# Forty zero products in TensorE's stream, an earlier memset, and a new written order, in an attention and feed-forward kernel

## The chip, the cores and the metric

The kernel runs on one core of one Trainium2 chip. The metric is the device time of one execution in microseconds, the median of several runs. The core has five engines, each with an instruction stream that it executes in order: TensorE (PE in the profile; its weight loads are shown apart as PEld), VectorE (DVE), ScalarE (ACT), GpSimd (POOL) and SyncE (SP). In this kernel POOL does little more than issue loads, SP issues transposes by DMA and stores.

## The reference: what is computed

Attention with a relative-position bias over 8 batches t, 8 heads, 576 positions and head size 64, and then a feed-forward layer over all 4608 positions:

```python
scores = scale * np.matmul(q, k.transpose(0, 1, 3, 2))   # (8, 8, 576, 576), head size 64
scores = scores + bias.transpose(2, 0, 1)[None, :, :, :] # by |distance| bucket and head
attn = softmax(scores)                                   # over the last axis
x = np.matmul(attn, v)  ->  (8 * 576, 512)               # heads side by side
h = x @ w_in                                             # (4608, 2048)
s = np.sin(alpha * h)
g = h + s * s / (alpha + 1e-09)
return g @ w_out                                         # (4608, 512), float32
```

The inputs are float32; the kernel works in float16 with float32 sums.

## The kernel before

**Tiles and stages.** Heads go in pairs p = 0..3, queries of a batch in two windows w of 256 and a rest of 64. The task names used below are those of the source; the digits are t, p, w, half, or block and slice.

- `n` (L581) loads a pair's k or q in natural order through POOL, casting it to float16; `t` (L703) turns it on TensorE, and `c` copies it to the tile kT or qT on DVE or ACT. The first pair comes in two halves by its own loads (`r`), casts (`f`, L653 on DVE or L651 on ACT), turns (`th`, L688) and copies (`ch`). From t = 3 on, k and q are staged in float16 in DRAM (`g`, L608, POOL) and turned by a DMA transpose on SP (`k`, L614). `v` (L587) and `y` (L593) load the values.
- `T` (L766) makes a group of four score products into two banks of PSUM; `X` (L720, L725, L749) and `S` do it for the rest of 64. `E` is the exp on ACT (L774), `B` the product with the bias band on DVE, `A` (L805, L810) and `L` (L821) the products with v, `N` the division (L842, L843). `Y` turns the result into the tile xT: for t = 0 on TensorE (`P`) with a copy, later by a DMA transpose on SP (L850, L861).
- The feed-forward layer goes in 9 blocks of 512 positions. `I` (L887) is one slice of 128 of the first product, four 128x512 products; `Z` (L893) the sine, `Q` the square, `G` (L905) the sum; `O` (L915) a piece of the second product, `W` the eviction and `D` the store. A block's `I` needs the `Y` of every batch that it covers.
- A bias table is made early: `bu`, `be`, `bs`, `bm`, `bc`, then `j` loads it as a band (tile toep, L662) on SP or POOL, and `m` makes masks from it.

**What sets the order.** One long string, ORDER, lists all tasks; `/` is followed by the engine, where it is not the first that the task allows (A is ACT, D is DVE, G is POOL), and the PSUM bank. `_planned` only checks it. Each engine's instructions come in exactly that order, and a task waits at its place for what it needs. The string begins:

```text
id/A r00 ms r10/A r01 n011 r11/A sub n020 cst tab al n021 n100 f00 n031 th00/7 f10/A ch00 n010 f01
th10/6 y00 th01/7 ch10 ch01/A T0000/0 v00 T0001/2 ET0000 n131 bu/7 ET0001 f11 t020/6 n030 be
```

Near the second batch's end it reads, around SP's transposes: `L2 ... Y23 ... YL2 ... Y20 ... k41 ... I2.0`.

**Cleared tiles.** Task `ms` (L569 to L578) writes constants on DVE: ones and zeros in the tiles of v and vt, and zeros in the two tiles kd. From t = 2 on, kd holds the last 64 columns of two heads' k as a block diagonal (`o`), so that one full product does for both heads.

Of the kernel before, what the change touches and what calls it, by code (L numbers as in the profile page):

```python
# [45 lines left out]
def _graph(K):  # L46
# [15 lines left out]
    ms = add("ms", "DVE", lambda e, b: K.memsets())  # L62
# [277 lines left out]
PE_X, KD = 1, 2  # L340
# [3 lines left out]
id/A r00 ms r10/A r01 n011 r11/A sub n020 cst tab al n021 n100 f00 n031 th00/7 f10/A ch00 n010 f01  # L344
th10/6 y00 th01/7 ch10 ch01/A T0000/0 v00 T0001/2 ET0000 n131 bu/7 ET0001 f11 t020/6 n030 be
th11/5 c020/A t021/4 bs n121 ch11 bm/7 c021/A n111 T0010/0 bc T0210/2 ET0010 j0 j2/G T0201/4
t011/7 ET0210 t010/6 j1/G c011 T0211/0 ET0201 T0200/2 j3 c010 at/7 n110 ET0200 av T0101/4 v03
t100/6 t031/7 ET0101 c100 t030/3 v01 t131/2 c031 ET0211 T0100/4 y01 c030 ET0100 v02 c131 T0300/0
X00r/6 ET0300 n101 BT0210 BT0200 T0110/2 t111/5 n231 BT0000 ET0110 T0011/0 n130 t121/4 BT0001 c111
ET0011 n200 X01r/2 BT0010 c121 m0 EX00r X00q/0 BT0201 BT0110 m1 BT0101 EX01r BT0100 X01q/4 wi1  # L350
T0311/6 BX00r EX01q BT0011 A000/3 n210 BT0300 A010/2 EX00q n220 N000 A001/5 m3 BT0211 ET0311
t110/4 N010 m2 t101/3 T0111/0 c110/A N001 T0301/6 n120 ET0111 BX01r T0310/4 c101 n230 A020/2
ET0301 BT0111 wi2 A021/3 N020 T1000/0 ET0310 wi0 S0/7 N021 t130/6 y11 t231/2 ET1000 BT0301 T1001/4
BX00q A011/3 BT0311 wi3 ES0 c231 c130/A X10r/0 y10 ET1001 A030/7 BT0310 N011 v12 P00/6 BS0 EX10r
P02/2 A031/3 N030 v11 BX01q T1011/4 Y02/A N031 t220/7 ET1011 n221 T1100/0 Y00 T1300/2 c220 P01/6
ET1100 P03/5 Y01 t120/4 BT1011 t210/7 ET1300 T1010/0 c120 L0/6 ET1010 Y03 wo0 t230/4 NL0 t200/5
T1311/2 c200 T1301/0 I0.8/6 ET1311 c230 ET1301 S1/5 c210 X11r/2 v10 I0.0/4 BT1000 EX11r BT1100 v13
I0.3/7 ES1 Z0.0 BS1 BT1010 I0.9/5 BT1300 PL0/3 I0.7/2 YL0 n211 Z0.9 Q0.0 I0.1/3 wo1 Z0.3 Q0.9 G0.0
Z0.7 I0.12/1 v21 Q0.3/A G0.9 I0.2/4 wo2 Z0.8 G0.3 Q0.7/A I0.5/5 n201 Q0.8 Z0.2 G0.7 I0.14/7 Z0.1
Q0.2 Q0.1/A G0.8 I0.10/2 Z0.12 wo3 G0.2 I0.13/6 Q0.12/A BX10r g31 G0.1 Z0.10 I0.4/4 BT1001 Z0.14  # L360
G0.12 A100/3 Q0.10/A Q0.14 I0.11/1 Z0.5 G0.10 g30 Z0.4 G0.14 I0.6/0 Q0.4/A BX11r Z0.11 N100
I0.15/7 G0.4 Q0.5/A y20 O0.0/3 Z0.6 G0.5 O1.0/2 g40 Q0.6/A O0.2 O0.4 Z0.15 G0.6 T1101/4 Z0.13 O1.2
Q0.11 ET1101 Q0.15 O0.6 G0.11 v22 A101/0 BT1301 O0.8 G0.15 A130/1 N101 O1.4 N130 Y10 O1.6 Q0.13
X11q/4 T1111/0 G0.13 t211/7 v20 ET1111 O1.8 c211 O0.10 y21 EX11q BT1111 T1200/0 O1.10 BT1311
ET1200 t201/7 t221/6 T1110/4 c221 T1201/0 ET1110 O1.12 BT1200 O1.14 ET1201 c201 O0.12 T1310/4 v23
W1 X10q/6 ET1310 T1210/0 BT1101 O0.14 BT1110 BX11q A110/2 BT1201 EX10q W0 A111/5 BT1310 D0 ET1210
N110 A120/4 N111 T1211/6 T2100/2 o2 T2110/0 ET1211 Y11 O3.0/5 BT1210 BX10q O3.2 ET2100 BT1211 O3.4
X20r/6 N120 ET2110 A131/3 S2/4 A121/2 EX20r N131 T2200/0 N121 O3.6 ES2 ET2200 BT2100 T2111/6 Y12
T2101/2 O2.0/4 ET2111 O3.8 X21r/0 ET2101 O3.10 Y13 O3.12 EX21r O3.14 T2000/2 k30 T2201/6 T2211/0
ET2000 O2.2 O2.4 ET2201 O2.6 O2.8 ET2211 BT2201 O2.10 BT2101 W3 T2001/2 T2210/6 T2010/0 BT2111  # L370
ET2001 D3 L1/5 BT2200 ET2010 I1.5/3 BX21r D1 v33 BX20r ET2210 T2310/0 v32 k31 I1.8/2 ET2310 y30
I1.1/7 Z1.5 g71 A210/6 I1.14/1 N210 Z1.8 NL1 I1.15/0 y31 Q1.8/A Q1.5 I1.0/6 G1.5 Z1.14 g50 Z1.1
I1.2/5 Q1.14 G1.8 Z1.0 I1.7/3 Q1.0/A BT2110 G1.14 v30 A220/2 G1.0 Z1.7 I1.13/1 g41 Q1.1/A N220
Z1.2 I1.6/6 G1.1 Q1.7/A Q1.2 I1.4/2 o3/A G1.7 Z1.6 I1.3/7 BT2000 Z1.4 G1.2 O2.12 Z1.15 O2.14 Q1.4
Q1.6/A I1.10/5 G1.4 g51 W2/A Q1.15 O5.0/3 Z1.3 G1.6 I1.12/4 Q1.3/A G1.15 Z1.13 I1.9/6 G1.3 Z1.10
O6.0/2 Q1.13 Z1.12 I1.11/7 G1.13 Z1.9 Q1.10 g60 X21q/0 Q1.9 Z1.11 O5.2 G1.10 EX21q O6.2 Q1.11 O5.4
BT2210 G1.9 A211/5 O5.6 G1.11 O6.4 BT2211 T2011/6 T2300/0 Q1.12 O6.6 ET2300 G1.12 O5.8 O6.8 N211
ET2011 O6.10 BT2010 Y21 BT2300 T2301/0 T2311/4 BT2011 T3110/6 O6.12 ET2311 BT2310 O5.10 BT2001
ET2301 O5.12 D2 O6.14 A200/5 ET3110 BT2301 O5.14 N200 W6/A T3300/0 YL1 T3011/6 W5 X20q/4 ET3300
A221/2 BS2 BT2311 O4.0/3 EX20q N221 O4.2 BT3300 T3301/0 ET3011 T3000/4 Y22 A201/2 BX21q ET3301  # L380
A230/7 N201 k40 A231/6 ET3000 N230 X30r/0 N231 O4.4 EX30r O4.6 BX20q T3001/4 L2/2 ET3001 Y23
T3101/0 NL2 v42 T3211/6 T3100/4 ET3101 O4.8 YL2 v41 O4.10 ET3100 O4.12 y41 O7.0/2 ET3211 BT3100
X31q/0 v31 T3111/4 O7.2 ET3111 Y20 g70 O7.4 O4.14 EX31q X30q/4 W4 T3201/6 O7.6 EX30q BT3011 k41
# [548 lines left out]
def kernel(  # L932
# [48 lines left out]
```

## Time and profile before

| | us |
|---|---|
| median of 3 runs | 381.02 |
| lowest and highest | 379.35, 384.81 |
| the profiled execution | 381.76 |
| its span, first to last instruction | 379.9 |
| PE, ACT, DVE, POOL busy in the span | 365.4, 310.5, 265.3, 86.0 |

The profile is one execution. A matmul's busy time is modelled from a pipeline, so a busy PE need not be at its peak. The slices are a fortieth of the span, 9.5 us, each; a digit is tenths of busy time, and for PEclk tenths of the full TensorE clock that was granted. In the list of waits a line gives who waited, what ended the wait, and us in total, times and longest. The chain follows the work that ended last back to the start; its rows give start, length and what was on it. In the timeline each row is a run of like instructions, with the idle time before it in brackets.

### The profile page before, as it was taken

The page shows a single profiled execution, that of the slowest core. Times are in us where ns is not written, and L with a number is a line of the kernel's source. Part 1 is how long each engine was busy: PE and PEld are TensorE (multiplying, and loading weights), DVE is VectorE, ACT ScalarE, POOL GpSimd, SP SyncE. Part 2 cuts the span into 40 slices and gives each one's busy share as a digit, 9 for nine tenths or more (in the row PEclk, how much of TensorE's full clock was granted, in tenths as well). Part 3 has the DMA queues.
Part 4 walks back from the last instruction along what each step waited for, and adds up shares of the span by engine and source line. Part 5 has one row for each costly group of instructions (what it writes and reads, how often), then busy time and mean ns, then how long its engine had stood idle before and what let it go on. Part 6 is the DMA issues. An engine that isn't in the chain of part 4 may idle for free.

```text
span 379.9 us, 9143 instructions
## 1 busy us (share of the span) xinstructions
PE 365.4 (96%) x3769; PEld 195.6 (51%) x3769; DVE 265.3 (70%) x613; ACT 310.5 (82%) x417; POOL 86.0 (23%) x104
## 2 busy tenths in 40 slices
PE   4879999999998899999999999999999999999996
PEld 3567445654464455544554555445654564444453
DVE  4789899639975496389754985596729866769412
ACT  5979998999899599899988989999899855686301
POOL 8894682048208000600000050500000000000000
PEclk9989999999999899999999999999999999999999
DMA  9999999999999992890254078980130032020005
GB/s 174 217 170 184 186 193 158 126 201 145 157 131 142 172 100 57 93 155 21 98 129 97 0 83 135 141 69 28 40 89 3 2 83 92 2 83 0 2 29 193
DMA packets 140889, 39.68 MB, mean 104 GB/s; under 512 B 126208, under 2 KB 136304, under 8 KB 140848
## 3 DMA queue, kind: packets, MB, share of 16 engines
q0 software_dynamic: 92864, 18.45, 60.0%
q1 hardware_dynamic: 46272, 18.61, 23.5%
q10 hardware_dynamic: 1712, 2.04, 1.6%
q8 instruction: 29, 0.48, 0.5%
q14 instruction: 12, 0.10, 0.1%
HBM read 36.89 MB, written 15.34 MB: 137 GB/s over the span
## 4 chain that ended last, share of the span: by engine, by line
PE 88%; DMA 6%; ACT 2%; POOL 1%; issue 1%; SPq 1%; DVE 1%; POOLq 0%
PE acc L915 33%; PE acc L887 31%; PE acc L810 8%; PE acc L766 8%; PE acc L805 2%; DMA xT<-xp 2%; DMA v<-in_v_dram 2%; PE acc L821 2%; DMA xT<-in_k_dram 2%; DMA toep<-e_sb 1%; ACT s L893 1%; PE acc L720 1%; PE acc L703 1%; POOL xT L581 1%; PE acc L749 1%
## 5 line engine op out<-in xcount | busy, mean ns | idle before, releaser
L915 PE MATMUL acc<-w_out,g 128*128 128x512 f16 (+1 forms) x592 | 144.3, 374 | 0.0
L887 PE MATMUL acc<-xT,w_in 128*128 128x512 f16 x576 | 135.8, 381 | 2.8 <-DMA xT<-xp 2.2
L774 ACT ACTIVATE u<-acc 128x1024 f16<-128x1024 f32 x128 | 123.7, 1034 | 12.2 <-PE acc L766 11.3
L893 ACT ACTIVATE s<-acc,alphaT 128x512 f16<-128x512 f32 x144 | 91.9, 682 | 23.6 <-PE acc L887 23.0
L905 DVE SCALAR_TENSOR_TENSOR g<-s,inv_a,acc 128x512 f16<-128x512 f16 x144 | 103.2, 742 | 7.3 <-ACT s L898 5.7
L887 PEld LDWEIGHTS <-w_in 128*128 128x128 f16 x576 | 55.3, 98 | 69.2 <-issue 6.5
L915 PEld LDWEIGHTS <-g 128*128 128x128 f16 x592 | 52.7, 98 | 59.0 <-issue 7.3
L797 DVE TENSOR_TENSOR u<-u,toep 128x256 f16<-128x256 f16 (+1 forms) x128 | 58.9, 489 | 19.8 <-ACT u L774 19.5
L587 POOL DMA_DIRECT2D v<-in_v_dram x32 | 30.9, 972 | 145.5 <-PE acc L821 79.0
L810 PE MATMUL acc<-v,u 128*128 128x65 f16 x1024 | 45.4, 196 | 0.5 <-DMA v<-in_v_dram 0.5
L900 DVE TENSOR_TENSOR s<-s 128x512 f16<-128x512 f16 x83 | 34.0, 419 | 17.0 <-ACT s L893 16.7
L810 PEld LDWEIGHTS <-u 128*128 128x128 f16 x1024 | 41.9, 99 | 4.9 <-issue 0.9
L766 PE MATMUL acc<-qT,kT 64*128 64x256 f16 x512 | 42.0, 278 | 1.5 <-DVE kT L653 1.0
L898 ACT ACTIVATE s<-s 128x512 f16<-128x512 f16 x61 | 37.9, 629 | 1.1
L653 DVE COPY outs<-acc 128x512 f32<-128x512 f32 (+1 forms) x24 | 16.2, 675 | 26.7 <-PE acc L915 25.4
L774 ACT ACTIVATE ux<-acc 128x1024 f16<-128x1024 f32 x32 | 32.4, 1035 | 1.8 <-PE acc L720 0.9
L766 PEld LDWEIGHTS <-kT 64*128 64x128 f16 x512 | 20.4, 96 | 22.8 <-issue 18.2
L842 DVE RECIPROCAL rden<-acc 128x4 f32<-128x4 f32 x72 | 12.7, 177 | 25.1 <-PE acc L810 18.7
L805 PE MATMUL acc<-vt,ux 128*128 128x130 f16 x128 | 28.8, 225 | 1.0 <-DMA vt<-in_v_dram 1.0
L843 DVE TENSOR_TENSOR xp<-acc,rden 128x256 f16<-128x256 f32 x64 | 27.2, 424 | 2.3
L651 ACT ACTIVATE outs<-acc 128x512 f32<-128x512 f32 (+1 forms) x13 | 7.6, 582 | 18.6 <-PE acc L915 18.5
L805 PEld LDWEIGHTS <-ux 128*128 128x128 f16 x128 | 12.7, 99 | 8.2 <-issue 2.8
(68 smaller groups left out, 199.2 us busy)
## 6 DMA issues: line engine op xcount, KB each, us to landing
out_dram<-outs SPq DMA_DIRECT2D x30, 256.0 KB, 2.3
v<-in_v_dram POOLq DMA_DIRECT2D x32, 128.0 KB, 6.8
staged_q<-in_q_dram POOLq DMA_DIRECT2D x5, 576.0 KB, 12.4
staged_k<-in_k_dram POOLq DMA_DIRECT2D x5, 576.0 KB, 14.9
w_in<-in_moe_w_in_dram POOLq DMA_DIRECT2D x4, 512.0 KB, 10.5
w_out<-in_moe_w_out_dram POOLq DMA_DIRECT2D x4, 512.0 KB, 10.6
xT<-in_q_dram POOLq DMA_DIRECT2D x11, 144.0 KB, 5.6
xT<-in_k_dram POOLq DMA_DIRECT2D x11, 144.0 KB, 5.9
```

What stands on the lines that cost most here:

```text
L587: self.nc.gpsimd.dma_start(out=self.vs[t % 2][:, c, :, 0:D], in_=src)
L766: self.nc.tensor.matmul(out=s[:, o:o + 256], lhsT=self.kT[t % 2][r, p, 128 * c:128 * c + 128], rhs=self.qT[t % 2][r, p, 256 * w:256 * w + ...
L774: self.nc.scalar.activation(out=c["u"], in_=c["s"], func=AF.Exp, scale=0.125)
L797: self.nc.vector.tensor_tensor(out=io, in0=io, in1=m, op=ALU.mult)
L805: nc.tensor.matmul(out=c["av"][:, 130 * j:130 * j + 130], lhsT=cx["u"][:, o:o + 128], rhs=vt[:, p, :], start=True, stop=True, skip_group_c ...
L810: nc.tensor.matmul(out=c["av"][:, 130 * j + 65 * a:130 * j + 65 * a + 65], lhsT=cells[ch // 2]["u"][:, o:o + 128], rhs=vv[:, ch, 2 * p + a ...
L887: self.nc.tensor.matmul(out=c["h"], lhsT=self.w_in[:, j, 128 * f:128 * f + 128], rhs=self.xT[:, j, 512 * b:512 * b + 512], start=(j == 0), ...
L893: self.nc.scalar.activation(out=c["s"], in_=c["h"], func=AF.Sin, scale=self.alphaT[:, f:f + 1])
L898: self.nc.scalar.activation(out=c["s"], in_=c["s"], func=AF.Square)
L900: self.nc.vector.tensor_tensor(out=c["s"], in0=c["s"], in1=c["s"], op=ALU.mult)
L905: self.nc.vector.scalar_tensor_tensor(out=self.g[b][:, f, :], in0=c["s"], scalar=self.inv_a[:, f:f + 1], in1=c["h"], op0=ALU.mult, op1=ALU ...
L915: self.nc.tensor.matmul(out=c["mo"], lhsT=self.g[b][:, f, 128 * (tau % 4):128 * (tau % 4) + 128], rhs=self.w_out[:, f, at], start=(f == 0) ...
```

## The change

Three things change. A new task `mz` clears the two kd tiles first, ahead of `ms`, which keeps the rest of the constants. Forty new tasks `F0` to `F39` on TensorE, which depend on `mz` alone, each multiply a cleared kd tile by itself into a free bank of PSUM, 512 columns wide; nothing reads the result. Depending on the task written before it on TensorE, a fill uses all of the array, one half of its rows, or half of its columns. And ORDER is written anew from its second word to its last: every engine's stream, the queues of SP and POOL and the banks follow another order, and some copies change between DVE and ACT (the first cast, f00, goes to ACT, the copy `bc` and the masks m0, m1, m3 to DVE).

```diff
-    ms = add("ms", "DVE", lambda e, b: K.memsets())
+    zero = add("mz", "DVE", lambda e, b: K.memset_kd())
+    ms = add("ms", "DVE", lambda e, b: K.memsets(), [zero])
+    for i in range(NFILL):
+        add(f"F{i}", "PE", lambda e, b: K.fill(b), [zero], bank=1)
...
-PE_X, KD = 1, 2
+PE_X, KD, NFILL = 1, 2, 40
...
+        self.form = "full"
...
+    def memset_kd(self):
+        for i in (1, 0):
+            self.nc.vector.memset(self.kd[i], 0.0)
...
-            self.nc.vector.memset(self.kd[i], 0.0)
+
+    def fill(self, bank):
+
+        z, o = self.kd[1], self.acc[:, bank, :]
+        if self.form == "rows":
+            z = z[64 * (bank % 2):64 * (bank % 2) + 64]
+        w = z[:, 0, 0:64] if self.form == "cols" else z[:, 0, :]
+        self.nc.tensor.matmul(out=o[0:64] if self.form == "cols" else o, lhsT=w,
+                              rhs=z[:, :, :].rearrange("p a n -> p (a n)"), start=True, stop=True)
...
+            if eng == "PE" and task.key[0] != "F":
+                k = task.key
+                rows = k[0] == "T" or k[0] == "X" and k[-1] == "q"
+                ops.form = "rows" if rows else "cols" if k[0] in "tL" else "full"
```

The new string begins as follows. It has six fills before the first turn, three more before the first score group T0000, 29 between that and the first A (A000), and two between A000 and the first product of the feed-forward layer, which is I0.2 in place of I0.8:

```text
id/A r00 mz r10/A r01 n021 ms F0/7 r11/A sub n011 F1/6 cst tab F2/7 al n020 F3/6 n010 F4/7 f00/A
F5/6 n031 th00/7 f10/A F6/6 n030 f01 th10/5 F7/6 n130 ch10 th01/4 ch00 F8/6 v01 ch01/A T0000/0
```

Around SP's transposes before block 2 it reads: `Y23 ... k40 ... Y22 ... k41 ... Y20 ... Y21 ... I2.10`, with v43, v40, g70 and g61 on POOL between Y20 and I2.10. Before block 7 it reads `Y73 ... I6.4 ... O22.14 ... L7 ... I7.3`.

More of the change, by code (lines that the diff above doesn't have):

```diff
@@ L349 @@
[L349 to L354, printed above, removed]
@@ L373 @@
[L373 to L378, printed above, removed]
@@ L379 @@
[L379 to L383, printed above, removed]
-S3/3 O7.8 g61 BT3000 ET3201 O7.10 BT3110 X31r/0 BX30r BX31q T3200/4 ES3 BT3001 EX31r T3010/6
@@ L460 @@
+O35.4a O35.8a D33 O32.14 O35.12a W32/A O35.4b W35a D32/A O35.8b D35a O35.12b W35b/A D35b/A
 """
```

216 lines of the change are left out of this document (117 added, 99 removed).

## The prediction

> **What bounds the kernel now.** I read the page first: the span and its 40 slices of 9.5 us each.
>
> ```profile
> span 379.9 us, 9143 instructions
> ...
> PE   4879999999998899999999999999999999999996
> ...
> PEclk9989999999999899999999999999999999999999
> ```
>
> TensorE is full but for two places: the first four slices, and a dip near slice 13. Both have a dip of the granted clock in or behind them. The list of PE's waits (us in total, times, longest) names them; its first row, 3.9 us, is the wait for the first load, shown below:
>
> ```profile
> PE acc L887 <- DMA xT<-xp: 2.2, 1, 2.2
> PE acc L805 <- DMA vt<-in_v_dram: 1.0, 1, 1.0
> ...
> PE acc L810 <- DMA v<-in_v_dram: 0.5, 1, 0.5
> ```
>
> The chain that ended last (start, length, what) says when PE becomes the bound:
>
> ```profile
> 1.29 3.26 POOL xT L581 x5
> ...
> 10.42 5.67 DMA toep<-e_sb
> ...
> 16.38 6.17 DMA v<-in_v_dram
> ...
> 22.59 0.45 PE acc L810 x6
> ...
> 25.34 0.44 PE acc L810 x8
> ...
> 28.22 0.24 PE acc L810 x8
> ...
> 29.33 0.63 PE acc L703 x24
> ...
> 36.22 0.74 PE acc L821 x34
> ...
> 118.21 6.32 DMA xT<-xp
> ...
> 165.34 11.22 PE acc L887 x52
> ```
>
> Up to 22.59 us the chain is POOL's loads: the last chunk of v for the first batch (t=0) holds the first A. After that it is nearly all TensorE. So the end moves by what changes before 22.59, by products added or taken behind it, and by the gap at 118 to 128. At full rate a 128x512 product is 11.22/52 = 0.216 us. The row at 25.34 shows A's products at 0.44 per eight, the row at 28.22 at 0.24: the stretch behind the v wait ran at half rate. The windows confirm it:
>
> ```profile
> 5.00:10.00 5.00, 4.57 (x62) 3.31 (x64) 1.63 (x5) 3.81 (x7) 4.28 (x7) 1.00 1.35 202
> 10.00:15.00 5.00, 4.64 (x99) 3.25 (x93) 3.03 (x7) 5.00 (x7) 4.42 (x7) 1.00 1.41 240
> 15.00:20.00 5.00, 3.58 (x64) 1.72 (x61) 4.89 (x11) 5.00 (x6) 4.35 (x8) 1.00 1.89 190
> 22.00:23.00 1.00, 0.46 (x10) 0.41 (x8) 1.00 (x3) 1.00 (x3) 1.00 (x3) 0.84 1.42 142
> 24.00:25.00 1.00, 1.00 (x21) 1.00 (x19) 1.00 (x3) 0.00 (x0) 0.92 (x3) 0.50 1.18 196
> 26.00:27.00 1.00, 1.00 (x32) 0.83 (x27) 0.96 (x4) 0.64 (x2) 1.00 (x2) 0.96 1.25 191
> 125.00:126.00 1.00, 1.00 (x5) 0.35 (x3) 0.00 (x0) 1.00 (x1) 0.00 (x0) 0.54 2.01 123
> 128.00:129.00 1.00, 1.00 (x5) 0.40 (x4) 1.00 (x3) 0.17 (x1) 0.00 (x0) 0.76 2.36 156
> ```
>
> (PE busy is the second figure, the granted clock the third from the end.) From the fractions the clock is 0.50 from about 22.7 to 26.1 and from about 125.1 to 128.5: 3.4 us each time, 1.7 us of products lost each time. A third half-rate stretch is hidden, because the clock column shows 1.00 there:
>
> ```profile
> 3.85 0.45 PE L688 MATMUL acc<-ident,xT 96*64 96x96 f16 x6 [3.85 <-DVE xT L653]
> 4.95 0.69 PE L688 MATMUL acc<-ident,xT 96*64 96x96 f16 x12 [0.65 <-ACT xT L651]
> 5.95 1.04 PE L766 MATMUL acc<-qT,kT 64*128 64x256 f16 x8 [0.31 <-DVE qT L653]
> ...
> 9.42 1.46 PE L766 MATMUL acc<-qT,kT 64*128 64x256 f16 x12
> 10.81 1.17 PE L703 MATMUL acc<-ident,xT 96*64 96x96 f16 x24
> ...
> 26.50 0.95 PE L766 MATMUL acc<-qT,kT 64*128 64x256 f16 x12
> ...
> 37.96 0.60 PE L887 MATMUL acc<-xT,w_in 128*128 128x512 f16 x2
> ```
>
> Twelve score products took 1.46 us at 9.4 and 0.95 at 26.5; 24 turns 1.17 at 10.8 against 0.63 at 29.33. So PE ran at half rate up to about 12 us.
>
> **The change part by part.**
>
> *Middle gap.* Y20's transpose was issued at 118.21 and landed 6.32 us later, and PE waited 2.2 for it, then ran 3.4 us at half rate: 2.2 + 1.7 = 3.9 us lost. SP's queue there, and the transposes of that line in general:
>
> ```profile
> 118.21 1.26 SPq L850 DMA_TRANSPOSE xT<-xp  x1
> 119.57 4.58 SPq L614 DMA_TRANSPOSE qT<-staged_q  x1
> ...
> DMA to landing us min/median/max: 2.4/2.5/7.3
> ```
>
> In the old order 3.8 us of PE work stood between Y20 and the first product of block 2 (I2.0), and 6.3 was needed. The new order puts Y20 7.8 us ahead of I2.10 and the last one, Y21, 5.9 us (sums of the pieces between at full rate: 0.43 for two products of L915, 0.3 for a score group from 0.95 for three, 0.6 for an A from 0.24 for eight of its eighteen products). But k41 now stands ahead of both on SP, 4.58 us of issue, and the loads of v for t=4, g70 and g61 start beside them. If the loads slow them as before, Y21 lands about 1 us late; at 2.5 it is early by 3. I take 0.4 late, so this part gives -3.5, between -3.9 and 0.
>
> *The other transposes.* The last one before each later block stands 2.0 to 5.9 us of PE work ahead, against 2.4 to 6.0 in the old order (Y20's 3.8 apart), where the shortest made no wait that the list shows. The shortest now is Y73: two products of L915, four of L887 and L7 before I7.3, 0.43 + 0.86 + 0.74 = 2.0 (L7 at the 0.74 of the row at 36.22), against 2.5 to land. I take +0.4 for all, between 0 and +2.2, the one wait known.
>
> *The fills.* Forty products, 40 x 0.216 = 8.6 us of PE at full rate, 0.43 each at half. PE executes them in their place whether anything waits or not. Six stand ahead of the first turn: they need only the cleared tile, whose memset is now the first on DVE, before those of v and vt. The first cast moves from DVE to ACT:
>
> ```profile
> 0.82 0.11 DVE L572 MEMSET v<- 128x64 f16 x1 [0.82 <-PEq L965]
> ...
> 1.70 0.27 DVE L578 MEMSET kd<- 128x256 uint32 x1
> ...
> 2.66 1.28 ACT L651 ACT_TABLE_LOAD   x1 [2.66 <-issue]
> ...
> 3.44 0.36 DVE L653 CAST xT<-toep 96x384 f16<-96x384 f32 x1 [0.35 <-DMA toep<-in_k_dram]
> ...
> 4.38 0.52 ACT L651 ACTIVATE xT<-toep 96x384 f16<-96x384 f32 x1 [0.43 <-DMA toep<-in_q_dram]
> ```
>
> The tile is clear at 0.82 + 0.27 = 1.1, and 6 x 0.43 = 2.6 ends by 3.9, about the end of the first wait (3.85). ACT is free at 3.94, so the cast ends near 4.5 instead of 3.80: 0.65 later. Three fills at half rate (1.3) go into the two waits of 0.65 and 0.31 before the first score. First score: about 7.0 instead of 5.95.
>
> Between the first score (T0000) and the first A (A000) stand 29 fills, 6.3 us, and one more score group and turn, 0.6. Old stretch: 5.95 to 22.59 is 16.6 us. Its idle time is 0.43 + 0.36 + 1.42 from the windows less the 0.96 before 5.95, then 1.0 and 0.5 for vt and v: 2.8. Half rate from 5.95 to 12 costs 3.0. What is left, 10.8, is work at full rate. New stretch, if no wait is left and the clock is full from T0000: 10.8 + 6.9 = 17.7, so the first A at 24.7, 2.1 later than 22.59. Behind it, what stands before the first L887 product is even: two turns and one score group fewer (-0.9), one S0-like group and one X group more (+0.5), two fills (+0.4). If the fills keep the clock up, the 1.7 comes back. Net +0.4. I add 0.2 for half rate left after 7.0 and take +0.6. Ends: -0.4, when the first score is as early as now; +4, when the 2.8 us of waits lie elsewhere than planned and only half of the rest is gained.
>
> [...] The row first: no wait between 5.95 and 22.6 is longer than 1.0 us, and yet the clock fell at 22.7. [...]
>
> *Loads.* Ahead of the first A stand the same loads on POOL as before (11 turns' inputs, four v, two vt, two of toep), two of them now behind the wait of toep for e_sb: at 3.26/5 = 0.65 to issue, up to 1.3 later than now, so 23.9. The fills' 24.7 covers it. The first w_in piece wanted is again the second in the queue. Cost nothing; if the fills were free, 1.3 would show.
>
> *ACT and DVE.* The same evictions; m0, m1, m3 and the copy to e_sb move to DVE. Before 38 us an exp takes 0.93 (ten in 9.27):
>
> ```profile
> 10.07 9.27 ACT L774 ACTIVATE u<-acc 128x1024 f16<-128x1024 f32 x10
> ```
>
> Twenty of them end with the last of t=0 at 7.5 + 18.6 + 0.7 of other work = 26.8; the As run from 24.7 on and the last takes its exps at about 32: covered.
>
> **Sum.** Profiled execution 381.76 us (span 379.9 and 1.9 around it): 381.76 - 3.5 + 0.4 + 0.6 = 379.3. The median of the three runs shown, 381.02, is 0.7 lower, so **378.5**. Behind the first L887 product the work is the same in both orders, product for product, and the switches of ACT's table are eight pairs in each; nothing else moves the end.
>
> **The rivals.**
>
> 1. *The front gains too.* The first score comes early, no wait is left, loads and clock allow it: -0.4 for +0.6, nothing for transposes, -3.9: 381.0 - 3.9 - 0.4 = 376.7, and with 1.3 of small waits beyond it 375.4. For: ACT sat idle from 24 to 25 (its 0.00 in the windows) and would no longer. Against: 6.3 us of fills before the first A for 2.8 us of waits.
> [...]
> 3. *The gap moves*: Y20 and Y21 behind k41, or Y73, arrive 2 us late and the clock halves again: +3.5, 382.0. For: 11 us of transposes and loads beside them. Against: 5.9 us of distance.
> 4. *Slower.* PE is the bound from the first score to the first A, and each fill behind an operand that is already there costs its 0.216: it decides from the point where more than 2.8 us of waits and 3.0 of half rate are asked for. With the old waits still there and half rate to 12 us, 2.8 + 3.0 on top of 379.3 less 0.7: 384.4; with the gap of rival 3 as well, 388. For: room 5.8, need 6.9. Against: PE near-busy from 1.2 us should have its full rate by 8, since it came after 6 us of work from 5.95.
>
> That the change does nothing at all is not open: the fills are in PE's stream.
>
> **How the numbers follow.** Forecast (376.9 to 379.7) 0.47; rival 1 0.14; rival 2 0.12; rival 3 0.16; rival 4 0.11. Range 375.0 to 385.0: from rival 1's end to rival 4's first figure. Faster by over 2% is under 373.4, below every sum here, left 0.06 for what I do not see; slower by over 2% is over 388.6, rival 4 with the gap, 0.07; within 2%, about what a measurement of this kernel tells from no change, 0.87.
>
> **What would show it.** L887's first product at 38 to 39 us; the clock 1.00 from 8 us on, and no 0.50 at 22 to 26 nor at 125 to 128; the wait of L887 for xT under 0.5 us; in PE's waits no v. Wrong if the first L887 product comes after 40, if a wait for xT over 2 us stands before any block, or if the clock halves more than once after 10 us.

## The result, and the profile after

| | before | changed |
|---|---|---|
| median, us (6 executions each) | 380.44 | 385.27 |
| lowest and highest, us | 378.57, 384.81 | 383.32, 387.32 |
| the profiled execution, its span, us | 381.76, 379.9 | 387.32, 385.5 |

The ratio is 1.0136, with a 95% interval of 1.0104 to 1.0169: the changed kernel is 1.4% slower, 4.8 us by the medians, where the forecast had it 2.5 us faster. The median lies just above the end of the range, 385.0. Medians here and below are over all executions of a kernel; the ratios leave out the few that ran in a slower state of the chip. The profiled execution of the changed kernel is the slowest of its six.

In the changed kernel the lines stand lower in the file: L905 is the first expert product (L887 before), L828 and L823 the two products of A (L810, L805), L784 the scores (L766), L721 the turns (L703), L605 and L611 the loads of v and vt (L587 and L593), L839 the products of task L (L821), L933 the second expert product (L915), L792 the exp (L774), and L595 the fills. In the kernels of the experiments the numbers move by a few more, as the string ORDER wraps differently; the tiles tell which instruction it is. The page of the changed kernel, span and PE:

```profile
span 385.5 us, 9222 instructions
...
PE   8988999999999999999999999979999999999995
...
PEclk9999999999999999999999999989999999999999
```

The dip at slice 13 is gone, and there is a new one at slice 27, in PE and in its clock. The list of PE's waits names it:

```profile
PE acc L828 <- DMA v<-in_v_dram: 3.8, 3, 2.1
PE acc L595 <- DVE kd L577: 1.2, 1, 1.2
PE acc L721 <- issue: 0.9, 1, 0.9
PE acc L784 <- ACT qT L669: 0.8, 1, 0.8
```

No wait of L905 for xT is left: the middle gap was closed, with its 2.2 us of waiting and its half clock. In its place stand waits for v: the 3.8 us of the list are two waits at 250 us and one of 0.98 in the front. PE's timeline at 250 (start, length, what, and in brackets the wait before it):

```profile
250.62 0.19 PE L828 MATMUL acc<-v,u 128*128 128x65 f16 x1
252.87 0.22 PE L828 MATMUL acc<-v,u 128*128 128x65 f16 x2 [2.06 <-DMA v<-in_v_dram]
253.82 0.31 PE L828 MATMUL acc<-v,u 128*128 128x65 f16 x5 [0.73 <-DMA v<-in_v_dram]
...
255.44 3.27 PE L933 MATMUL acc<-w_out,g 128*128 128x512 f16 x8
```

That is A620, the A of batch t=6, and it stands 2.8 us for pieces of v; the eight products behind it take 3.27 us where eight at 0.216 take 1.7. POOL's timeline shows why v came so late:

```profile
194.44 0.62 POOL L611 DMA_DIRECT2D vt<-in_v_dram  x1 [32.58 <-PE acc L839]
195.04 1.78 POOL L605 DMA_DIRECT2D v<-in_v_dram  x2
238.16 0.64 POOL L611 DMA_DIRECT2D vt<-in_v_dram  x1 [41.34 <-PE acc L839]
238.79 1.77 POOL L605 DMA_DIRECT2D v<-in_v_dram  x2
240.53 0.66 POOL L611 DMA_DIRECT2D vt<-in_v_dram  x1
241.15 4.42 POOL L605 DMA_DIRECT2D v<-in_v_dram  x5
```

The new order writes, on POOL, `y60 v53 v60 y71 v72 v71 y61 v73 v62 v61 v63`. The load y71 refills a buffer of t=5 and has to wait for `L5` (L839), 41.3 us. y61, v62, v61 and v63, which could go at 197, stand behind it. All of them leave between 240.5 and 245.6, in a crowd with t=7's, and the chain of waits has the last of t=6 landing 10.03 us after its issue, at 253.8.

The other place is the front. The first expert product:

```profile
38.82 0.36 PE L721 MATMUL acc<-ident,xT 96*64 96x96 f16 x8 [0.90 <-issue]
...
40.77 1.47 PE L905 MATMUL acc<-xT,w_in 128*128 128x512 f16 x6
```

It came at 37.96 before and comes at 40.77: 2.8 us later, although no half clock is left in the front (the clock is full from 9.1 us on).

**The balance of the two profiled executions**, 387.32 - 381.76 = 5.6, is an estimate, good to some tenths: PE's time against its pieces at full rate, summed up over the trace, changed less before: +2.6 by 60 us, -3.9 from there to 140 (the 2.2 and 1.7 of the middle gap), +0.9 from 140 to 240, +4.8 from 240 to 260 (2.06 + 0.73 of waits, 1.6 by the eight slow products, 3.27 - 1.7, and some around them), +0.6 to the last product and +0.5 behind it. Two stretches carry it, the front and the late gap; the 0.9, 0.6 and 0.5 lie in no single place.

### The profile page after: what moved, and what is told of

Read it like the earlier page. It is cut to its first block, busy times and chain, and to the rows that moved or that the text cites. A ratio compares the mean times of both kernels' runs of the same rounds, so it can differ in the third digit from the quotient of the medians.

```text
span 385.5 us, 9222 instructions
## 1 busy us (share of the span) xinstructions
PE 373.6 (97%) x3809; PEld 196.4 (51%) x3809; DVE 266.0 (69%) x617; ACT 313.6 (81%) x419; POOL 84.1 (22%) x98
## 4 chain that ended last, share of the span: by engine, by line
PE 70%; issue 13%; DMA 5%; ACT 4%; DVE 4%; POOL 3%; ACTq 0%; POOLq 0%; DVEq 0%
PE acc L933 28%; PE acc L905 22%; PE acc L784 7%; PE acc L828 6%; DMA v<-in_v_dram 4%; ACT u L792 2%; DVE g L923 2%; PE acc L823 2%; POOL v L605 2%; PE acc L738 1%; PE acc L839 1%; ACT s L911 1%; PE acc L767 1%; DMA out_dram<-outs 1%; DVE xp L861 1%
## 5 line engine op out<-in xcount | busy, mean ns | idle before, releaser
L933 PE MATMUL acc<-w_out,g 128*128 128x512 f16 (+1 forms) x592 | 146.0, 377 | 0.0
L905 PE MATMUL acc<-xT,w_in 128*128 128x512 f16 x576 | 135.3, 380 | 0.0
L792 ACT ACTIVATE u<-acc 128x1024 f16<-128x1024 f32 x128 | 123.8, 1033 | 13.1 <-PE acc L784 11.7
L905 PEld LDWEIGHTS <-w_in 128*128 128x128 f16 x576 | 54.9, 98 | 65.0 <-issue 2.3
L933 PEld LDWEIGHTS <-g 128*128 128x128 f16 x592 | 52.8, 98 | 58.6 <-issue 9.7
L815 DVE TENSOR_TENSOR u<-u,toep 128x1024 f16<-128x1024 f16 (+1 forms) x128 | 58.3, 484 | 20.6 <-ACT u L792 20.1
L828 PE MATMUL acc<-v,u 128*128 128x65 f16 x1024 | 44.0, 193 | 3.8 <-DMA v<-in_v_dram 3.8
L605 POOL DMA_DIRECT2D v<-in_v_dram x32 | 34.7, 1132 | 49.9 <-PE acc L828 24.1
L784 PE MATMUL acc<-qT,kT 64*128 64x256 f16 x512 | 43.2, 274 | 1.4 <-ACT qT L669 0.8
L828 PEld LDWEIGHTS <-u 128*128 128x128 f16 x1024 | 40.2, 97 | 8.6 <-issue 4.3
L918 DVE TENSOR_TENSOR s<-s 128x512 f16<-128x512 f16 x80 | 32.7, 420 | 16.0 <-ACT s L911 15.6
L916 ACT ACTIVATE s<-s 128x512 f16<-128x512 f16 x64 | 39.3, 629 | 1.1
L611 POOL DMA_DIRECT2D vt<-in_v_dram x16 | 13.0, 811 | 100.7 <-PE acc L839 93.6
L860 DVE RECIPROCAL rden<-acc 128x4 f32<-128x4 f32 x72 | 12.8, 178 | 31.3 <-PE acc L828 25.7
L792 ACT ACTIVATE ux<-acc 128x1024 f16<-128x1024 f32 x32 | 32.7, 1032 | 1.5 <-PE acc L738 0.8
L784 PEld LDWEIGHTS <-kT 64*128 64x128 f16 x512 | 20.4, 94 | 25.3 <-issue 22.4
L671 DVE COPY outs<-acc 128x512 f32<-128x512 f32 (+1 forms) x22 | 14.9, 676 | 23.6 <-PE acc L933 23.3
L823 PE MATMUL acc<-vt,ux 128*128 128x130 f16 x128 | 28.3, 221 | 0.0
```

The lines of the kernel that those rows point to most:

```text
L605: self.nc.gpsimd.dma_start(out=self.vs[t % 2][:, c, :, 0:D], in_=src)
L784: self.nc.tensor.matmul(out=s[:, o:o + 256], lhsT=self.kT[t % 2][r, p, 128 * c:128 * c + 128], rhs=self.qT[t % 2][r, p, 256 * w:256 * w + ...
L792: self.nc.scalar.activation(out=c["u"], in_=c["s"], func=AF.Exp, scale=0.125)
L815: self.nc.vector.tensor_tensor(out=io, in0=io, in1=m, op=ALU.mult)
L823: nc.tensor.matmul(out=c["av"][:, 130 * j:130 * j + 130], lhsT=cx["u"][:, o:o + 128], rhs=vt[:, p, :], start=True, stop=True, skip_group_c ...
L828: nc.tensor.matmul(out=c["av"][:, 130 * j + 65 * a:130 * j + 65 * a + 65], lhsT=cells[ch // 2]["u"][:, o:o + 128], rhs=vv[:, ch, 2 * p + a ...
```

## The experiments

The sixteen kernels below differ from one of the two in ORDER and in the number of fills, or join the two orders; the fills compute nothing that an output needs, so none of them leaves out work. Times are medians in us, and ratios are to the kernel before, measured beside it on the same chip. The experiments did not all run on one chip, so one is best compared with another by the ratios.

**The late loads and the fills (four kernels).** First the changed kernel with the loads of t=6 ahead of those of t=7:

```diff
-y60 v53 v60 y71 v72 v71 y61 v73 v62 v61 v63
+y60 v53 v60 y61 v62 v61 v63 y71 v72 v71 v73
```

> The changed kernel, with y61, v62, v61 and v63 (values of t=6) moved on POOL from behind v71 and v72 to just after v60. Theory (POOL's order): they stood behind loads that wait for L5, came late, and A620 waited 2.8 us for them at 250 to 254, in the profiled run with half a clock behind it. Now no wait for v there, first L887 product unchanged at 40.8, median 3 to 4.5 below the changed kernel's 385.3: 381 to 382. Rival (DMA rate: the loads take that long wherever they are issued, or the loss is elsewhere): a wait of 2 us or more stays, median 384.5 to 386.

Measured: 383.36 (ratio 1.0070, 1.0039 to 1.0100), and on POOL

```profile
196.72 0.66 POOL L610 DMA_DIRECT2D vt<-in_v_dram  x1
197.34 2.67 POOL L604 DMA_DIRECT2D v<-in_v_dram  x3
```

The four loads go 44 us sooner. The windows from 250 to 260 (the window, its length, then busy time and instructions of PE, PEld, DVE, ACT and POOL, the granted clock, DMA share and GB/s), of the changed kernel and then of this one:

```profile
250.00:260.00 10.00, 7.21 (x43) 3.06 (x42) 5.84 (x13) 6.43 (x11) 0.00 (x0) 0.83 0.97 106
```

```profile
250.00:260.00 10.00, 9.78 (x114) 5.44 (x111) 8.89 (x22) 9.26 (x14) 0.00 (x0) 1.00 0.01 2
```

The gap and its half clock are gone and nothing takes their place. So the cause is shown; it is worth 1.9 us by the medians (385.27 to 383.36), 0.7% of the 1.4%. That is less than the 3 to 4.5 us expected from the profile. The mean granted clock of the executions says why in part: it is 0.998 to 1.0 in all twelve of this kernel and 0.993 to 0.999 in the six of the changed one. One half clock of 3.4 us takes 1.7/383 = 0.0044 off that mean, so only three of the six can have had a whole one.

Then the changed kernel without any fill, with the first fourteen only, and without F6 to F13 (which stand around the first scores):

```diff
-PE_X, KD, NFILL = 1, 2, 40
+PE_X, KD, NFILL = 1, 2, 0
```

(14 and 32 in the other two; the fills left out are struck from ORDER.)

> The changed kernel without its forty fills, everything else in place. Theory (the fills delay the front by the bias chain, and give back the clock): copy to e_sb ends near 10.5 instead of 11.9, the first A gets its v 1.5 us earlier, but the clock halves once between 15 and 28 (1.7): first L887 product at 39.5 to 41, median 384 to 386. Rival 1 (the fills are pure cost on PE's path): first L887 product at 37 or earlier, median 379 to 381. Rival 2 (the fills carry more than they cost): first product after 42, median 387 or more.

> The changed kernel with its first fourteen fills alone (F0 to F13, up to the bias product); the other 26 are gone. Theory (fills between 11 and 24 us keep the clock): the clock falls to 0.50 for one window between 14 and 28 us, first L887 product 0 to 2 us later than 40.8, median 385 to 387. Rival (the clock stays by itself, the 26 only fill waits): granted clock 1.00 throughout the front, first product within 0.5 of 40.8, median 384.5 to 385.5. If the 26 are on the path, first product before 39 and median under 383.

> The changed kernel without the eight fills between the first turn and the bias product (F6 to F13). Theory (these run at half rate, 0.43 each, and hold up the bias product, POOL's loads of toep behind it, and the v behind those): copy to e_sb ends 1 to 2.5 us earlier, the last v of t=0 lands at 23 to 24 instead of 25.1, first L887 product at 39 to 39.8, median 383.5 to 384.5. Rival (what holds the front is ACT and DVE after the first A): v earlier, but the first product within 0.4 of 40.8, median 385. Rival 2 (POOL's order alone): v lands within 0.5 of 25.1.

| fills | median | ratio (interval) | first score | first expert product | half clock in the front |
|---|---|---|---|---|---|
| 40 (changed kernel) | 385.27 | 1.0136 (1.0104 to 1.0169) | 6.8 | 40.8 | none after 9.1 |
| none | 384.95 | 1.0116 (1.0084 to 1.0148) | 6.4 | 41.0 | 17.1 to 20.5, 23.9 to 27.3 |
| F0 to F13 | 384.92 | 1.0137 (1.0091 to 1.0182) | 6.7 | 40.0 | 15.7 to 19.1, 22.6 to 26.0 |
| all but F6 to F13 | 386.36 | 1.0148 (1.0112 to 1.0185) | 6.5 | 40.6 | none after 12.4 |

In these profiles the clock stays full with the later fills and halves twice without them. But the time is the same to 0.4%, and the first expert product stands at 40 to 41 with or without; the theory that F6 to F13 hold it up by 1 us or more falls. Without fills TensorE has 3.2 us of waits between its first score and the first A, and two half clocks, 1.7 us each; with forty it has 0.08 us of waits there. What waits and clock give, the fills' own products take. So the 2.8 us of the front come with the new order even without a fill.

**The middle gap alone.** The kernel before, with only Y20 moved in SP's and DVE's order, to right behind `N201`:

```diff
-A230/7 N201 k40 A231/6 ... ET3111 Y20 g70 O7.4
+A230/7 N201 Y20 k40 A231/6 ... ET3111 g70 O7.4
```

> The kernel before, with one word moved: Y20 stands right after N201, ahead of k40, Y23 and YL2 on SP. Theory (the gap at 122 to 128 is Y20 queued behind two late transposes and slowed by loads beside it): it is issued before 115, the wait of 2.2 us and the half clock behind it go, 3 to 4 us in all: median 376.5 to 378 against 380.7. Rival (another operand of block 2 is as late, or the delay moves to k40 and the scores of t=4): wait of 1.5 us or more there or later, median 379.5 to 381.

Measured: 377.93, ratio 0.9934 (0.9901 to 0.9966): faster than both kernels. The wait for xT is gone, and with it the half clock. But behind it stood another wait, for v of t=3, in the list of waits and in PE's timeline:

```profile
PE acc L808 <- DMA v<-in_v_dram: 2.3, 2, 1.5
```

```profile
122.20 0.19 PE L808 MATMUL acc<-v,u 128*128 128x65 f16 x1
123.92 0.37 PE L808 MATMUL acc<-v,u 128*128 128x65 f16 x7 [1.53 <-DMA v<-in_v_dram]
```

In the kernel before it ended under Y20's. On POOL, v31 (at 116.42) stood behind v42, v41 and y41, which wait for t=2's work:

```profile
114.01 1.79 POOL L585 DMA_DIRECT2D v<-in_v_dram  x2 [16.04 <-PE acc L819]
115.79 0.64 POOL L591 DMA_DIRECT2D vt<-in_v_dram  x1
116.42 0.89 POOL L585 DMA_DIRECT2D v<-in_v_dram  x1
```

It is the late gap's mechanism, in the kernel before. So v31 was moved as well:

```diff
-v42 ... v41 ... y41 ... v31
+v31 v42 ... v41 ... y41
```

> The kernel before with Y20 early (as in the run with Y20 alone) and, on POOL, the load v31 moved ahead of v42, v41, y41, which wait for the A blocks of t=2 and held it back. Theory (a load that need not wait stood behind loads that must): the wait of A300 for v of t=3, 1.69 us at 122 to 124, goes, nothing else moves, no half clock after 14 us; 376.0 to 377.0, against 377.9 for Y20 alone. Rival (v31 is late by its own buffer or by the DMA's load at 110 to 120, not by its place): the wait of A300 stays over 1 us, 377.5 to 378.5. Second rival (the wait hides another behind it, as Y20's wait hid this one): the gap at 122 goes and over 1 us turns up at the next block's A, 377.5 to 378.5.

Measured: 377.46, ratio 0.9911 (0.9886 to 0.9937), the best version found. v31 goes 19 us sooner, and PE is busy through the window, which held 8.47 of 10 with Y20 alone:

```profile
97.38 1.40 POOL L585 DMA_DIRECT2D v<-in_v_dram  x1
```

```profile
118.00:128.00 10.00, 10.00 (x104) 5.23 (x103) 8.02 (x23) 9.85 (x13) 3.87 (x3) 1.00 1.84 153
```

The mechanism is shown. The gain of this second move, 0.5 us by the medians and 0.2% by the ratios, is inside the intervals; its profile also has a half clock at 21.4 to 24.8 that the other one's had not. Both moves together are clear of them: 3.5 us less than the kernel before measured beside it (380.96).

**Fills in the old order.** Y20 early, kd cleared first, and six fills right ahead of the first A:

```diff
-id/A r00 ms ... BT0011 A000/3
+id/A r00 mz ms ... BT0011 F0/3 F1/3 F2/3 F3/3 F4/3 F5/3 A000/3
```

> The kernel of e5 (order of before, Y20 early), with the kd tiles cleared first and six fills, all of them right before A000, where PE waits for v. Theory (fills that stand in a real wait cost nothing and keep the clock): no half clock at 22 to 26, first A still at 22 to 23, first L887 product at 36.3 to 37.3 instead of 38.0, median 1 to 1.7 below e5. Rival 1 (the clock falls by the waits before that): half clock stays, median as e5. Rival 2 (the 1.7 goes into new waits for ACT, as in the changed kernel): clock full, first product at 37.5 or later, median within 0.6 of e5.

Measured: 383.13, ratio 1.0059 (1.0020 to 1.0099): 5 us slower than without them. Its profiled execution took 380.47, 2.0 more than that of Y20 alone. The clock is full from 13.3 us on, but so it is, from 13.9, in the profile of Y20 alone, so there was no half clock to win back. The first A comes at 22.95 instead of 21.84 and the first expert product at 38.2 instead of 37.5, and at A400, 163 us, there is a new wait for vt:

```profile
PE acc L820 <- DMA vt<-in_v_dram: 1.5, 1, 1.5
```

0.7 and 1.5 account for the 2.0, not for the 5: the executions spread from 379.7 to 386.2 (one, at 616.33, apart), and where the slower ones lose is open. Nothing speaks for fills.

**What delays the front: three guesses on loads and casts.** All start from the changed kernel with t=6's loads first (383.36). One moves the loads of the first A's v ahead of the wait for the bias band on POOL, one the two loads n110 and n100, one puts the first cast back on DVE:

```diff
-... v01 ... y00 ... j0 j1 ... y01 ... v00 ... v02 ... v03
+... v01 ... y00 y01 v00 v02 v03 ... j0 j1 ...
```

> The kernel of e1 (changed, values of t=6 moved forward), with y01, v00, v02 and v03 moved on POOL ahead of j1. Theory (the first A waits for v, whose loads stand behind the wait of toep for the bias copy): the last v of t=0 lands near 18 instead of 25.1, no wait of the first A for it, first L887 product 1 to 2 us earlier than 40.7, median 381.5 to 382.5 against e1's 383.4. Rival (behind the first A the exps, copies and bands of ACT and DVE set the pace, or the turns whose loads are now later): first product within 0.6 of 40.7, median 383 or more.

```diff
-... y00 ... j0 j1 ... n110 ... n100
+... y00 n110 n100 ... j0 j1
```

> The changed kernel with v of t=6 first (383.4) and the n loads n110 and n100 moved ahead of the toep wait j1 on POOL, right after y00, where the order before had its counterparts. Theory that these two loads behind the wait delay the front: the first L905 product 39 to 40 (40.7 without the move), the end 381.5 to 382.5. Rival (the front is set by the sum of the loads and by ACT's casts, and one load sooner makes another later): the first L905 product 40.3 to 41.5, the toep loads or v of t=0 land 0.5 us later, 383 to 384.5.

```diff
-f00/A
+f00
```

> The changed kernel with v of t=6 first (383.4) and the first cast f00 put back on DVE, as in the order before (the changed order has f00 and r10 both on ACT ahead of the turns). Theory that the late first score (6.7 against 5.95) starts the front's loss: the first score 5.9 to 6.2, the first L905 product 39.8 to 40.2, 382.4 to 383. Rival (the first score is not on the front's path, the loads are): the first score sooner by 0.4 or more, the first L905 product still at 40.5 to 41, 383 to 384. Third (DVE, which has ms and mz first, is no sooner with it): the first score 6.6 or later, no change.

| moved ahead | median | ratio (interval) | last v of t=0 landed | first A | first expert product |
|---|---|---|---|---|---|
| nothing | 383.36 | 1.0070 (1.0039 to 1.0100) | 25.1 | 25.4 | 40.7 |
| v of t=0 | 385.85 | 1.0141 (1.0103 to 1.0179) | 18.9 | 27.4 | 43.4 |
| n110, n100 | 383.75 | 1.0082 (1.0056 to 1.0107) | 23.0 | 26.3 | 41.8 |
| f00 on DVE | 382.42 | 1.0031 (1.0010 to 1.0052) | 25.6 | 26.4 | 42.9 |

The first two moves did to the loads what they should, and the front came later each time: with v early, the turns' inputs wait, and PE stands 1.7 us for an eviction that comes late with them:

```profile
24.93 0.71 PE L594 MATMUL acc<-kd 64*128 64x512 f16 x3 [1.67 <-DVE kT L670]
```

So an earlier v alone does not bring the front forward. The third made the first score no sooner (6.96); the lower median and the later first product of its profile, one of its slowest executions, contradict each other, and it decides nothing. The later fronts of the last two have another cause that these moves did not aim at, the time at which TensorE came to its full rate; it is shown below.

**Joining the two orders.** The old order to P00 (about 32 us) and then the new one, and the mirror of it, the new order to T1000 and then the old one:

```diff
-old order, whole
+id/A r00 ms ... BT0310 N011 v12 P00/6 (old) | n221 n201 t120 c120 t221 ... (new, what is left of it)
```

```diff
-new order, whole
+id/A r00 mz ... N001 T1000/2 BT0300 wi1 (new) | n231 n210 A021 N021 ... (old, what is left of it)
```

> The old written order up to P00 (about 32 us), and from there the changed order with v of t=6 first; no filling products; seven turns keep another PSUM bank where the two orders meet. Theory (the changed kernel's late front comes from its written order before 32 us, loads and casts and turns together): the first L905 product at 37 to 38.5 as in the kernel before, no wait for xT near 120, none for v near 250, 380 to 381. Rival (what is late comes from after 32 us, where the new order asks for its qT and kT sooner than ACT has them, or from any order that is not the old one): the first L905 product at 39.5 to 41, 382.5 to 384.

> The mirror: the changed order with 38 of its filling products up to T1000 (about 28 us), and from there the old order with Y20 early and v31 ahead (377.5 with the old front). Theory (the late front comes from the changed order before 32 us): the first L905 product at 40 to 41.5, nothing of it won back behind, 379.5 to 381. Rival (the front's delay is of the stretch behind 28 us): the first L905 product at 38 to 39.3, 377.5 to 379.

Measured: 395.80 (ratio 1.0398, 1.0358 to 1.0438) and 394.01 (1.0351, 1.0298 to 1.0403). Neither theory is tested: each join opened a gap, since a turn behind the seam needs a load that its own order had issued early and the other front had not. The load stands behind the w_in loads, 512 KB each. The first join's PE timeline:

```profile
42.57 0.69 PE L701 MATMUL acc<-ident,xT 96*64 96x96 f16 x12 [10.05 <-DMA xT<-in_q_dram]
```

The second one's list of waits:

```profile
PE acc L720 <- DMA xT<-in_q_dram: 11.2, 1, 11.2
```

With the loads issued ahead, in the first join and in the second:

```diff
-wi1 n210 n220 ... P00/6 n221 n201
+wi1 n210 n221 n201 n220 ... P00/6
```

```diff
-n120 n121 n220 wi3 ... wi1 n231 n210
+n120 n231 n210 n121 n220 wi3 ... wi1
```

> The join of the old order up to P00 and the changed order behind it again, with the two loads that came 10 us late at the seam (n221 and n201) issued ahead, right after n210, before the w_in loads. Theory (the late front comes from the changed order before 32 us): no gap over 2 us at the seam, the first L905 product at 37.5 to 39, 380 to 382. Rival (it comes from behind 32 us): the first L905 product at 40 to 41.5, 382.5 to 385. If another gap over 2 us opens at the seam, the join tells nothing of the front, and the sum of the waits behind 60 us alone is read.

> The mirror: the changed order with 38 filling products up to T1000, behind it the old order with Y20 early and v31 ahead, and the two loads that came late at the seam (n231 and n210) issued right after n120, before the w_in loads. Theory (the late front comes from the changed order before 28 us): no gap over 2 us at the seam, the first L905 product at 40 to 41.5, 380 to 381.5. Rival: the first L905 product at 37.5 to 39.3, 377 to 379.3.

Measured: 386.79 (1.0172, 1.0127 to 1.0218) and 388.97 (1.0223, 1.0190 to 1.0257), first expert products at 45.3 and 46.1. The waits at the seam are smaller (1.5 and 3.4 us), but many, so the joins say nothing of the split. They show how much of an order's time is the fit between its loads and its turns.

**What sets the front: a lead, and what it leaves open.** Counting score evictions on ACT (u and ux, 0.93 us each) gave the lead. The changed kernel's ACT:

```profile
7.48 1.02 ACT L792 ACTIVATE u<-acc 128x1024 f16<-128x1024 f32 x1 [0.56 <-PE acc L784]
...
9.32 1.02 ACT L792 ACTIVATE u<-acc 128x1024 f16<-128x1024 f32 x1
...
11.15 7.52 ACT L792 ACTIVATE u<-acc 128x1024 f16<-128x1024 f32 x8 [0.21 <-PE acc L784]
18.52 2.98 ACT L792 ACTIVATE ux<-acc 128x1024 f16<-128x1024 f32 x3
21.39 1.95 ACT L792 ACTIVATE u<-acc 128x1024 f16<-128x1024 f32 x2
23.33 1.02 ACT L792 ACTIVATE ux<-acc 128x1024 f16<-128x1024 f32 x1
24.25 1.02 ACT L792 ACTIVATE u<-acc 128x1024 f16<-128x1024 f32 x1
```

The kernel before (its ten at 10.07 are shown in the prediction):

```profile
6.60 1.94 ACT L774 ACTIVATE u<-acc 128x1024 f16<-128x1024 f32 x2 [0.51 <-PE acc L766]
...
19.21 3.80 ACT L774 ACTIVATE ux<-acc 128x1024 f16<-128x1024 f32 x4
22.83 1.10 ACT L774 ACTIVATE u<-acc 128x1024 f16<-128x1024 f32 x1
```

Both run without a pause from their long row on, but it starts at 11.15 instead of 10.07. The 17th eviction ends at 25.27 instead of 23.93. The guess that this row sets the front was put to the test in the best version, in both directions: four early evictions of turns (c011, c010, c100, c031, 0.65 us each) moved from DVE to ACT, and one (c021) from ACT to DVE.

```diff
-c011 ... c010 ... c100 ... c031
+c011/A ... c010/A ... c100/A ... c031/A
```

> The best version so far (old order, Y20 early, v31 ahead: 377.5, first L905 product at 37.0) with four early evictions (c011, c010, c100, c031; some 0.65 us each) moved from DVE to ACT, so that ACT starts its row of score evictions 2 us later and DVE has 3 us less. Theory (ACT's scores from 10 us on set the front: where ACT has done less of them by 15 us the first L905 product comes later): the first L905 product at 38.5 to 39.7, 379 to 380.5. Rival (DVE sets it as much, or the loads do): the first L905 product at 36.5 to 37.7, 376.5 to 378.

```diff
-c021/A
+c021
```

> The same version with one early eviction (c021, 0.65 us) moved from ACT to DVE, which is idle then. Theory (ACT's scores set the front): the first L905 product 0.3 to 0.7 sooner, 36.3 to 36.8, and 376.5 to 377.2. Rival (the eviction comes later on DVE and the next score with it, or ACT is not the bound): 36.9 to 37.6, 377.2 to 378.

Measured: four more on ACT 381.28 (1.0018, 0.9992 to 1.0045), one fewer 378.55 (0.9938, 0.9915 to 0.9962), against 377.46 (0.9911, 0.9886 to 0.9937) without either. Four more are slower, by 3.8 us of the medians and clear of the intervals. One fewer is inside them: neither a loss nor the theory's gain is shown. The two profiles, each of the slowest execution of its kernel, say less of ACT than they seem to, because both lost time at a place that the moves do not touch. The load that the turn at 7.3 us needs is the second on POOL in all three kernels, issued at 2.0, and it landed at 7.3, 8.8 and 9.05. TensorE at that turn, in the best version, with four more on ACT, and with one fewer:

```profile
7.34 0.69 PE L701 MATMUL acc<-ident,xT 96*64 96x96 f16 x12
```

```profile
8.83 0.69 PE L701 MATMUL acc<-ident,xT 96*64 96x96 f16 x12 [1.14 <-DMA xT<-in_k_dram]
```

```profile
9.09 0.69 PE L701 MATMUL acc<-ident,xT 96*64 96x96 f16 x12 [1.10 <-DMA xT<-in_k_dram]
```

One fewer is 1.75 us late here and 2.1 late at its first expert product. With four more, TensorE also ran at half rate until 25.6 us, instead of 11.1, and paused 1.74 us in its own issue before 37.6. So the front of neither profile can be put down to the eviction that was moved.

Over the kernels with an undivided order, from their ACT timelines (profiled executions, us):

| kernel | 17th score eviction ends | first expert product | between |
|---|---|---|---|
| old order, Y20 and v31 early | 23.7 | 37.0 | 13.3 |
| before | 23.9 | 38.0 | 14.0 |
| old order, six fills | 24.3 | 38.2 | 13.9 |
| old order, Y20 early | 24.4 | 37.5 | 13.1 |
| old order, one fewer on ACT | 25.5 | 39.1 | 13.6 |
| old order, four more on ACT | 28.1 | 43.5 | 15.4 |
| changed | 25.3 | 40.8 | 15.5 |
| changed, F0 to F13 | 25.3 | 40.0 | 14.8 |
| changed, all but F6 to F13 | 25.7 | 40.6 | 14.9 |
| changed, no fills | 25.9 | 41.0 | 15.1 |
| changed, t=6 first | 26.9 | 40.7 | 13.9 |
| the same, n110 and n100 ahead | 27.7 | 41.8 | 14.1 |
| the same, f00 on DVE | 27.9 | 42.9 | 15.1 |
| the same, v of t=0 ahead | 28.2 | 43.4 | 15.3 |

A late first column mostly goes with a late second one, but they can also part: the changed kernel and the one with t=6 first have the same order until 190 us, and the same first expert product with the 17th eviction 1.6 us apart; and the old order with one fewer on ACT has the changed kernel's first column and a second one 1.7 us sooner. So that ACT's row sets the front is not shown.

TensorE's own rows say more. The windows of the changed kernel (columns as above):

```profile
5.00:10.00 5.00, 5.00 (x47) 2.60 (x47) 1.94 (x6) 2.49 (x5) 3.03 (x5) 1.00 1.24 203
10.00:15.00 5.00, 5.00 (x113) 3.25 (x110) 4.41 (x9) 4.79 (x7) 2.99 (x6) 1.00 1.26 179
15.00:20.00 5.00, 5.00 (x56) 2.12 (x50) 4.83 (x14) 5.00 (x7) 5.00 (x8) 1.00 1.17 169
```

With the fills TensorE is full: its waits from the first score (6.83) to the first A (23.86) come to 0.08 us, where the kernel before has 3.03. So it hardly waits for ACT in this stretch. And in the kernels with this order and all forty fills the first A follows the time at which the products reach their full rate. Eight score products, in the changed kernel and in the one with n110 and n100 ahead:

```profile
10.72 0.61 PE L784 MATMUL acc<-qT,kT 64*128 64x256 f16 x8
```

```profile
11.78 1.04 PE L783 MATMUL acc<-qT,kT 64*128 64x256 f16 x8
```

| kernel | full rate from | waits, first score to first A | first A |
|---|---|---|---|
| changed | 9.1 | 0.08 | 23.9 |
| t=6 first | 12.7 | 0.17 | 25.4 |
| the same, f00 on DVE | 14.0 | 0.41 | 26.4 |
| the same, n110 and n100 ahead | 14.1 | 0.32 | 26.3 |

The first A comes 1.6 us later where half rate lasts 3.6 longer, and 2.5 later where it lasts 5: about half, which is what half rate costs an engine that is full. (The kernel with v of t=0 ahead is left out: it has 3.6 us of waits there, most of them for loads and for what hangs on them.)

Of the changed kernel's 2.8 us, then, 2.1 are there at the first A (23.86 against 21.76). From there to the first expert product it takes 16.91 us instead of 16.20: 2.64 of waits instead of 0.56, and 0.3 of other work, less the 1.7 of the half clock that is gone. The waits are 0.98 for v, 0.76 for a turn's eviction that ACT has late, and 0.90 in PE's own issue before 38.82, quoted above (the kernel before has such a pause, 0.62, behind its first expert product).

```profile
32.63 0.61 PE L784 MATMUL acc<-qT,kT 64*128 64x256 f16 x7 [0.76 <-ACT qT L669]
```

Without fills, other things take the same time: the 3.2 us of waits before the first A, 3.1 of them for ACT and DVE, and the two half clocks. Why the new order, freed of its fills, is no faster there than the old one is not settled.

## Why the prediction was wrong

**The middle gap** was right: -3.9 against -3.5. Y20 moved alone gave 1.9 us by the medians beside each other (379.81 to 377.93), less than the trace's 3.9. A wait of 1.5 us for v31 stood hidden behind it; with v31 moved too, it is 3.5 (380.96 to 377.46). And the sum took one profiled execution for the usual one. Its mean granted clock is 0.991, which is two half clocks. Of the 93 executions of the kernel before that the ratios of the experiments rest on, 21 are like it, 32 are at about 0.995, one half clock, and 40 at 0.999 or 1.0, with none. "The other transposes", +0.4: none was late.

**"Behind the first L887 product the work is the same in both orders, product for product, ... nothing else moves the end"** is the step that failed worst. The products are the same, but the loads are not: POOL's queue was followed in the front only. A wait was there to be read in ORDER: y71 needs `L5`, and t=6's loads stand behind it. It cost 4.8 us in the profile, 1.9 in the median. The list of what would show it had "in PE's waits no v", and this wait is the first row of that list.

**The fills** were put at +0.6 for the whole front, with ends of -0.4 and +4; it was +2.8, within the ends. From the first score to the first A the mechanism was right: TensorE without a wait, 17.7 us by the sum, 17.0 measured (6.83 to 23.86). The sum has a slip in it. From the idle time of the window 5 to 10 it takes the waits of 0.65 and 0.31, but the first of them ended at 4.95, outside that window; the old waits were 3.4 us and not 2.8, and with 3.4 the sum comes to 17.1. What failed is the stretch behind. There the sum counts the 1.7 us of clock as won back. They were, but waits that it put at nothing took them again: 0.98 for v, where "The fills' 24.7 covers it" stood; 0.76 for a turn's eviction on ACT, where "covered" stood, since the exps alone were asked whether they end in time; and 0.90 in TensorE's own issue. In the place of +0.6 by fills and clock stand +2.1 at the first A and +0.7 behind it.

**"Cost nothing"**, of the loads, held but for that 1 us: the last v of t=0 landed at 25.1 where the sum had 23.9, and the first A stood 0.98 us for it, as it had stood 0.5 before; but moving v forward made the front later, not sooner.

**The rivals.** Rival 4, the slow one, had a number near the measured one (384.4), by luck. TensorE is full from the first score to the first A, as it says, but its price, the old waits on top of the fills, did not come: the waits are gone, 1.9 us of the loss lie at 250, and without a single fill the kernel is as slow. Rival 2, 0.12 of the chances, had the clock fall all the same at the first A. It did not: in the changed kernel's profile it is 1.00 from 20 to 30 us, where the kernel before has 0.77 and 0.89 in the two halves of that stretch, and without the fills it halves at 17.1 and at 23.9. Rival 3 had the right kind of event, a gap that moves and halves the clock again, at the wrong place and with the wrong load: v at 250, not Y20 or Y73.

## What to carry to other kernels

When an order is written anew, follow every queue from end to end, not only where the change has its reason: a load that needs nothing, behind one that waits 41 us for a buffer, is a gap of 4 us, and it can be read in the order before anything runs. Closing one gap uncovers the next one that ended under it, so read what ends second. Filling an engine's idle time makes it full, and then its own rate sets the time: with forty fills the first A came 1.6 to 2.5 us later where TensorE's full rate came 3.6 to 5 us later. And one profiled execution is not the usual one: ask how many executions have the half clock that is to be won back.

## What the runs showed of the hardware

- **With the products of zeros the clock mostly stayed full.** With all forty, the changed kernel's profile has no half clock from 9.1 to 254 us; without, two before 28. Over the executions, the mean granted clock is 0.998 to 1.0 in all twelve of the changed kernel with t=6 first, 0.993 to 0.999 in the six of the changed kernel, and 0.987 to 1.0 in the six without fills, only one of them at 1.0. With v of t=0 ahead, and the 1.67 us of wait before 24.93, forty fills did not keep it: 0.66 from 25 to 30 us.
- **The clock halved without a long wait.** The windows of the kernel with F0 to F13 only, two of 5 us and the 3.4 us ahead of each fall:

```profile
15.00:20.00 5.00, 4.35 (x56) 1.92 (x54) 4.86 (x13) 5.00 (x6) 5.00 (x8) 0.66 1.29 176
20.00:25.00 5.00, 3.50 (x77) 2.72 (x72) 4.75 (x13) 4.67 (x6) 4.92 (x9) 0.76 1.68 159
12.30:15.70 3.40, 2.49 (x47) 1.43 (x42) 3.33 (x9) 3.40 (x5) 3.40 (x7) 1.00 0.82 199
19.20:22.60 3.40, 2.01 (x60) 1.55 (x57) 3.36 (x9) 3.40 (x5) 3.32 (x6) 0.99 2.11 158
```

PE was busy 2.49 and 2.01 of 3.4 us ahead of the falls at 15.7 and 22.6, more than half of the time, and idle for 0.91 and 1.39 us in all. In the kernel before it was busy 1.44 of the 3.4 us ahead of the fall at 22.7, where its longest wait was 1.04, and 2.96 of those ahead of 19.3, when the clock stayed full. Each half clock lasted 3.4 us, and in the run with F0 to F13 half, full and half followed each other at 15.7, 19.1, 22.6 and 26.0. What makes the clock fall, and at how much idle time, no run here shows.
- **Fills from 1.2 us on did not bring the full rate sooner with any certainty.** With F0 to F5 it came at 9.1 us in the changed kernel and at 12.4 to 14.1 in four others (all but F6 to F13, t=6 first, the same with f00 on DVE, the same with n110 and n100 ahead); with v of t=0 ahead PE made 64 products in 3.74 us of busy time from 5 to 10 us, where the changed kernel made 47 in 5.00. Without these fills at the start it came at 11.1 (Y20 and v31 early) to 13.9 us (Y20 early), and at 25.6 with four evictions more on ACT.
- **PE paused in its own issue** once or twice between 32 and 42 us in fourteen of the eighteen profiles, 0.4 us (Y20 and v31 early) to 1.7 (four more on ACT) with nothing that it waits for in the records. What it is stays open.
